# An mLSTM cell feeding a SwiGLU block: TensorE's order written out by hand, and the running maximum fetched by DMA

## The chip, the cores and the metric

The kernel runs on one core of a Trainium2 chip. The metric is the device time in microseconds of one execution. Before the change it was 806.16 us (median of 3 runs, 801.5 to 810.28). The core's engines are TensorE (PE, whose weight loads appear apart as PEld), VectorE (DVE), ScalarE (ACT), GpSimd (POOL) and SyncE (SP), which here issues DMAs.

## The reference

Two blocks follow each other. The first is an mLSTM cell over 4 batches, 8 heads, 768 time steps and a head width of 40, with a running maximum `m` that keeps the exponentials bounded:

```python
for t in range(S):
    m_new = np.maximum(f_gate[:, :, t] + m, i_gate[:, :, t])
    f_stab = np.exp(f_gate[:, :, t] + m - m_new)
    i_stab = np.exp(i_gate[:, :, t] - m_new)
    C = f_stab * C + i_stab * outer(v_t, k_t)
    n = f_stab * n + i_stab * k_t
    y[:, :, t] = sigmoid(o_t) * (C @ q_t) / max(|n . q_t|, 1)
```

The second takes the cell's output as 3072 tokens of width 320 and computes `(silu(x @ w_gate) * (x @ w_val)) @ w_out` with a hidden width of 1536. Everything is float32, except that the three weight matrices arrive as float64.

## The kernel before

**The cell** works in chunks of 128 time steps: 4 batches of 6 chunks, 24 chunks ("units") `u`. Inside a chunk the recurrence becomes matrix products. A chunk passes through `turn` (transposes `tp_kq` of k and q on TensorE; the copy `v_w` of v weighted for the state), `scores` (`sp`, k times q for each head, and a multiplication by the weights `w`), `attend` (`inter`, the state times q; `add`, the chunk's contribution to the state; `intra`, scores times v; their sum `y`), `rows` (the denominator `den`, and `x`, doubled into `xx_sb`) and `seam` (transposes `tp_x` that write x into `xT`). Heads lie in pairs, one in partitions 0 to 63 and one in 64 to 127, so `sp` contracts over 64 rows; it handles the four pairs of one half, and then the four of the other.

**The weights** `w` of a chunk are exp(g - M) under a causal mask, where M is the running maximum found by a scan on VectorE. M must stand in all 128 partitions. `weigh(b)` does that for a whole batch with 48 TensorE products `nm` over 32 rows; VectorE adds g, GpSimd masks, ScalarE takes the exponential.

**The feed-forward** works on half a batch, 384 tokens, at a time. `hidden` computes one of 12 slices of the hidden width: ten products `gv_ps` over 64 rows each, alternately for the gate (partitions 0 to 63) and the value (64 to 127); a sigmoid on ScalarE and two multiplications on VectorE follow. `project` multiplies by `w_out` for 128 tokens: 12 products `o_ps` over 128 rows. A float32 product is two instructions in the trace, a transpose one, so a `hidden` step is 20 rows of `gv_ps` there and a projection 24 of `o_ps`.

**The float64 weights** are converted on the chip in 18 pieces (`weight`), 12 of them for the gate and value and 6 for the output matrix: two raw loads or one, five operations on VectorE, a square on ScalarE, an addition on GpSimd. Three raw buffers turn over.

**Order.** The first batch of the cell is emitted with the conversions between its stages. After that the feed-forward of batch b is emitted with the cell of batch b+1 spread evenly between its steps. A scheduler then places the instructions of every engine, TensorE's too, by its own estimates of when each can run; every engine executes its list in order. SP issues the loads of k, q, v, o and the stores of the result from one in-order list; ScalarE's list issues the raw weight loads.

PSUM is split into four buffers for the cell (`cell`) and four for the feed-forward (`gen`).

Of the kernel before, what the change touches and what calls it, by code (L numbers as in the profile page):

```python
# [9 lines left out]
F32 = mybir.dt.float32  # L10
U32 = mybir.dt.uint32
# [3 lines left out]
PSUM = bass.MemoryType.PSUM  # L15

L = 128
# [4 lines left out]
def kernel(  # L22
# [19 lines left out]

    nc = tc.nc
# [8 lines left out]
    TW = S // 2  # L52
    HP = 64
    NKC = DM // HP
    assert NKC * HP == DM and NB * L == S and NFC * 128 == DF and TW % 128 == 0 and TW <= 512 and D <= DP and BH <= 128

    const = ctx.enter_context(tc.tile_pool(name="const", bufs=1))
    wpool = ctx.enter_context(tc.tile_pool(name="wpool", bufs=1))
    dpool = ctx.enter_context(tc.tile_pool(name="dpool", bufs=NB + 1))
    work = ctx.enter_context(tc.tile_pool(name="work", bufs=2))  # L60
    xtp = ctx.enter_context(tc.tile_pool(name="xtp", bufs=2))
    gsp = ctx.enter_context(tc.tile_pool(name="gsp", bufs=3))
# [10 lines left out]
    NR = 3  # L73
    kq_ring = [const.tile([128, 2, H, DP], F32, name=f"kq{r}") for r in range(NR)]
    v_ring = [const.tile([128, H, D1], F32, name=f"va{r}") for r in range(NR)]
    for r in range(NR):
        nc.vector.memset(kq_ring[r][:, :, :, D:], 0.0)
        nc.gpsimd.memset(v_ring[r][:, :, D:], 1.0)

    units = {}  # L80
    NU = B * NB

    def load(u):
        if u >= NU:
            return
        b, c = divmod(u, NB)
        un = units[u] = {"kq": kq_ring[u % NR], "v": v_ring[u % NR]}
        un["o"] = work.tile([128, H, D], F32, name="o_sb", bufs=NR)

        def src(a):  # L90
            return a[b, :, ts(c, L), :].rearrange("h p d -> p h d")

        nc.sync.dma_start(out=un["kq"][:, 0, :, 0:D], in_=src(k))
        nc.sync.dma_start(out=un["kq"][:, 1, :, 0:D], in_=src(q))
        nc.sync.dma_start(out=un["v"][:, :, 0:D], in_=src(v))
        nc.sync.dma_start(out=un["o"], in_=src(o_gate))

    for u in range(NR - 1):
        load(u)
# [9 lines left out]
    nid = const.tile([BH, BH], F32)  # L109
    nc.vector.tensor_scalar(nid, idb, scalar1=-1.0, scalar2=None, op0=ALU.mult)  # L110
# [8 lines left out]
    own = const.tile([128, 2 * D1], F32)  # L119
    nc.gpsimd.memset(own, 0.0)  # L120
    for two in range(2):
        nc.gpsimd.memset(own[two * DP:(two + 1) * DP, two * D1:(two + 1) * D1], 1.0)
# [3 lines left out]
    step = gates.tile([BH, NB, L], F32)  # L126
    nc.gpsimd.memset(step, 0.0)
# [5 lines left out]
    F_sb = gates.tile([BH, NB, L], F32)  # L133
    nc.vector.tensor_tensor_scan(flat(F_sb), flat(keep), flat(f_sb), 0.0, op0=ALU.mult, op1=ALU.add)
    g_sb = gates.tile([BH, NB, L], F32)
    nc.vector.tensor_sub(g_sb, i_sb, F_sb)
    nc.vector.tensor_copy(step[:, 1:, 0:1], F_sb[:, 0:NB - 1, L - 1:L])
    M_sb = const.tile([BH, NB, L], F32)
    nc.vector.tensor_tensor_scan(flat(M_sb), flat(step), flat(g_sb), NEG, op0=ALU.add, op1=ALU.max)
    m_in = gates.tile([BH, NB - 1, 1], F32)  # L140
# [24 lines left out]
    gates_scope.close()  # L165

# [6 lines left out]
    def weight(dst, src):  # L173
        if src[0][1].dtype == F32:
            for r, s in src:
                nc.scalar.dma_start(out=dst[r], in_=s)
            return
        shape = list(dst.shape)
        n = 1
        for x in shape[1:]:  # L180
            n *= x
        p = shape[0]

        def tmp(name, dt):
            return conv.tile([128, NPW], dt, name=name)[0:p, 0:n]

        raw = conv.tile([128, 2 * NPW], U32, name="raw", bufs=3)[0:p, 0:2 * n]
        for r, s in src:
            nc.scalar.dma_start(out=raw[r].rearrange("p (a d) -> p a d", a=shape[1]), in_=s.bitcast(U32))
        words = raw.rearrange("p (n two) -> p n two", two=2)  # L190
        lo, hi = words[:, :, 0], words[:, :, 1]

        top = tmp("top", U32)
        nc.vector.tensor_scalar(top, hi, scalar1=3, scalar2=0x3FFFFFFF, op0=ALU.logical_shift_left, op1=ALU.bitwise_and)  # L194
        nc.vector.scalar_tensor_tensor(top, in0=hi, scalar=0xC0000000, in1=top, op0=ALU.bitwise_and, op1=ALU.bitwise_or)  # L195
        size = tmp("size", F32)
        nc.scalar.activation(size, hi.bitcast(F32), AF.Square)
        nc.vector.scalar_tensor_tensor(top.bitcast(F32), in0=size, scalar=1.21 * 2.0 ** -30, in1=top.bitcast(F32),  # L198
                                       op0=ALU.is_ge, op1=ALU.mult)

        power = tmp("power", U32)
        nc.vector.tensor_scalar(power, top, scalar1=0xFF800000, scalar2=None, op0=ALU.bitwise_and)
        nc.vector.scalar_tensor_tensor(size, in0=lo, scalar=2.0 ** -52, in1=power.bitcast(F32),  # L203
                                       op0=ALU.mult, op1=ALU.mult)
        sz, tf = (x.rearrange("p (a d) -> p a d", a=shape[1]) for x in (size, top.bitcast(F32)))
        nc.gpsimd.tensor_tensor(dst, tf, sz, op=ALU.add)  # L206

    pieces = []
    for f0 in range(0, DF, PW):
        src = [(slice(i * HP, (i + 1) * HP), w[:, f0:f0 + PW].rearrange("(c p) f -> p c f", p=HP))  # L210
               for i, w in enumerate((moe_w_gate, moe_w_val))]
        pieces.append((wgv_sb[:, :, f0:f0 + PW], src))
    for m in range(0, NFC, 2):
        src = moe_w_out[m * 128:(m + 2) * 128].rearrange("(a p) d -> p a d", p=128)
        pieces.append((wo_sb[:, m:m + 2, :], [(slice(0, 128), src)]))


    w_tiles = {}

# [197 lines left out]
```

## Time and profile before

| what | value |
|---|---|
| profiled execution, its own time | 804.57 us |
| its span, first to last instruction | 802.8 us |
| mean granted TensorE clock | 0.947 |
| PE busy | 750.8 us (94%) |
| DVE busy | 329.1 us (41%) |
| ACT busy | 161.8 us (20%) |
| POOL busy | 132.4 us (16%) |
| HBM read, written | 27.72 MB, 3.93 MB |

Lines such as `L339 PE MATMUL gv_ps<-xT,wgv_sb` name the line of the kernel, the engine, the operation, and output and inputs by the program's names. Busy time counts overlapping instructions once, and the mean duration of one does not. In a list in order of time, the first number is the start in microseconds from the span's beginning and the second the length. In a table of stretches each engine's busy time stands with the number of its instructions, and behind them the granted clock, the DMA engines' busy share and the GB/s.

### The profile page before, as it was taken

How to read it: one execution, taken by the hardware profiler on the slowest of the kernel's cores; microseconds unless marked ns; L12 is line 12 of the kernel's file. 1: busy time of each engine (PE TensorE's matmuls, PEld its weight loads, DVE VectorE, ACT ScalarE, POOL GpSimd, SP SyncE). 2: the span in 40 equal slices, each digit the busy share in tenths (PEclk: the TensorE clock that was granted, in tenths of full speed). 3: DMA queues.
4: the chain of work that ended last, by engine and by line, in shares of the span. 5: the costliest groups of instructions: out<-in, count | busy, mean ns of one | idle time of the engine just before them, and what ended most of it. 6: DMA issues, size and time to landing. Idle time of an engine off the chain costs nothing.

```text
span 802.8 us, 10446 instructions
## 1 busy us (share of the span) xinstructions
PE 750.8 (94%) x4293; PEld 549.6 (68%) x4293; DVE 329.1 (41%) x571; ACT 161.8 (20%) x292; POOL 132.4 (16%) x145
## 2 busy tenths in 40 slices
PE   3956687999999999999999999999999999999998
PEld 2855666697676667976677667966677667556665
DVE  4577799743431442333422442333413441230330
ACT  2322123232202220322201220322201210110110
POOL 1453344431110100210110100310111000000000
PEclk9999997559999999789999999689999999999999
DMA  9266676001120111001110121010110000000000
GB/s 136 58 113 114 115 172 172 18 9 33 26 41 25 34 30 37 17 9 33 33 42 18 33 42 33 9 25 18 33 42 9 1 1 17 9 1 17 9 1 25
DMA packets 113136, 32.34 MB, mean 40 GB/s; under 512 B 100736, under 2 KB 111488, under 8 KB 113088
## 3 DMA queue, kind: packets, MB, share of 16 engines
q1 hardware_dynamic: 103392, 19.87, 14.2%
q10 hardware_dynamic: 9696, 11.80, 6.2%
q8 instruction: 34, 0.56, 0.3%
q14 instruction: 14, 0.11, 0.0%
HBM read 27.72 MB, written 3.93 MB: 39 GB/s over the span
## 4 chain that ended last, share of the span: by engine, by line
PE 91%; DVE 4%; issue 1%; POOL 1%; ACT 0%; ACTq 0%; DVEq 0%; POOLq 0%
PE gv_ps L339 40%; PE o_ps L349 20%; PE nm L228 9%; PE intra L291 6%; PE sp L261 5%; PE tp_kq L250 3%; PE inter L271 3%; PE add L278 3%; PE tp_x L321 2%; DVE top L195 1%; POOL xx_sb L311 1%; DVE top L194 1%; DVE top L198 0%; DVE size L203 0%; POOL wgv_sb L206 0%
## 5 line engine op out<-in xcount | busy, mean ns | idle before, releaser
L339 PE MATMUL gv_ps<-xT,wgv_sb 64*128 64x384 f32 x1920 | 344.4, 497 | 0.0
L339 PEld LDWEIGHTS gv_ps<-xT,wgv_sb 64*128 64x128 f32 x1920 | 191.3, 190 | 117.5 <-issue 12.3
L343 DVE TENSOR_TENSOR sg<-sg,gv_ps 128x384 f32<-128x384 f32 x96 | 53.2, 554 | 286.5 <-ACT sg L342 286.5
L349 PE MATMUL o_ps<-wo_sb,h_sb 128*128 128x320 f32 x576 | 158.7, 435 | 0.0
L349 PEld LDWEIGHTS o_ps<-wo_sb,h_sb 128*128 128x128 f32 x576 | 108.3, 190 | 45.2 <-issue 1.1
L342 ACT ACTIVATE sg<-gv_ps 128x384 f32<-128x384 f32 x96 | 47.0, 489 | 241.6 <-PE gv_ps L339 241.6
L228 PE MATMUL nm<-M_sb,nid 32*128 32x128 f32 x384 | 76.0, 390 | 0.0
L228 PEld LDWEIGHTS nm<-M_sb,nid 32*128 32x128 f32 x384 | 74.9, 301 | 0.7 <-issue 0.3
L245 POOL TENSOR_TENSOR v_w<-va,w_sb 128x328 f32<-128x328 f32 x24 | 18.2, 761 | 244.1 <-PE add L278 206.6
L230 DVE TENSOR_TENSOR w_sb<-nm,g_T 128x512 f32<-128x512 f32 x48 | 33.2, 692 | 61.5 <-PE nm L228 61.5
L344 DVE TENSOR_TENSOR h_sb<-sg,gv_ps 128x384 f32<-128x384 f32 x96 | 53.2, 554 | 11.0 <-PE gv_ps L339 1.2
L291 PE MATMUL intra<-va,s_sb 128*128 128x41 f32 x384 | 52.7, 302 | 0.0
L261 PEld LDWEIGHTS sp<-qT,kT 64*128 64x128 f32 x384 | 44.6, 215 | 11.6 <-ACT qT L252 6.5
L291 PEld LDWEIGHTS intra<-va,s_sb 128*128 128x128 f32 x384 | 51.5, 215 | 1.1 <-DVE top L198 1.1
L261 PE MATMUL sp<-qT,kT 64*128 64x128 f32 x384 | 46.0, 309 | 4.3 <-ACT qT L252 4.3
L321 PE MATMUL tp_x<-ident,xx_sb 128*128 128x128 f32 x120 | 21.4, 318 | 30.5 <-POOL xx_sb L311 30.5
L308 POOL TENSOR_TENSOR x_sb<-o_sb,y_sb 128x320 f32<-128x320 f32 x24 | 22.6, 941 | 155.4 <-DVE y_sb L294 151.1
L321 PEld LDWEIGHTS tp_x<-ident,xx_sb 128*128 128x128 f32 x120 | 15.6, 160 | 41.1 <-POOL xx_sb L311 33.3
L232 POOL TENSOR_SCALAR_AFFINE_SELECT w_sb<-w_sb 128x1024 f32<-128x1024 f32 x24 | 27.6, 1152 | 80.1 <-DVE w_sb L230 80.1
L352 ACT COPY z_sb<-o_ps 128x320 f32<-128x320 f32 x24 | 10.2, 426 | 137.2 <-PE o_ps L349 137.2
L234 ACT ACTIVATE w_sb<-w_sb 128x1024 f32<-128x1024 f32 x24 | 25.4, 1057 | 54.7 <-POOL w_sb L232 54.7
L301 ACT ACTIVATE o_sb<-o_sb 128x320 f32<-128x320 f32 x24 | 11.2, 468 | 114.0 <-DMA o_sb<-in_o_gate_dram 114.0
(67 smaller groups left out, 495.6 us busy)
## 6 DMA issues: line engine op xcount, KB each, us to landing
kq<-in_k_dram SPq DMA_DIRECT2D x24, 160.0 KB, 3.0
kq<-in_q_dram SPq DMA_DIRECT2D x24, 160.0 KB, 3.1
va<-in_v_dram SPq DMA_DIRECT2D x24, 160.0 KB, 2.6
o_sb<-in_o_gate_dram SPq DMA_DIRECT2D x24, 160.0 KB, 2.5
raw<-in_moe_w_gate_dram ACTq DMA_DIRECT2D x12, 320.0 KB, 5.0
raw<-in_moe_w_val_dram ACTq DMA_DIRECT2D x12, 320.0 KB, 4.5
raw<-in_moe_w_out_dram ACTq DMA_DIRECT2D x6, 640.0 KB, 5.3
out_dram<-z_sb SPq DMA_DIRECT2D x24, 160.0 KB, 1.8
```

The source lines that it names most:

```text
L228: nc.tensor.matmul(nm[:, j, :], lhsT=nid[:, row:row + 1].to_broadcast([BH, 128]), rhs=M_sb[:, c, :], start=True, stop=True)
L230: nc.vector.tensor_tensor(w[:, two], nm, g2[:, two].unsqueeze(2).to_broadcast([128, PR, L]), op=ALU.add)
L232: nc.gpsimd.affine_select(wf, wf, compare_op=ALU.is_ge, fill=NEG, base=0, pattern=[[0, H], [1, L]], channel_multiplier=-1)
L234: nc.scalar.activation(wf, wf, AF.Exp)
L261: nc.tensor.matmul(sp[:, j, :], lhsT=un["kT"][r, j, :], rhs=un["qT"][r, j, :], start=True, stop=True)
L291: nc.tensor.matmul(intra[:, h, :], lhsT=un["s"][:, h % 2, h // 2, :], rhs=un["v"][:, h, :], start=True, stop=True)
L321: nc.tensor.transpose(tp[:, kc - k0, :], units[u]["x"][:, kc, :, :].rearrange("p a d -> p (a d)"), ident)
L339: nc.tensor.matmul(ps[i], lhsT=wgv_sb[r, kc, ts(m, 128)], rhs=xts[b][r, kc, ts(n, TW)], start=(kc == 0), stop=(kc == NKC - 1))
L342: nc.scalar.activation(sg, ps[0], AF.Sigmoid)
L343: nc.vector.tensor_tensor(sg, sg, ps[0], op=ALU.mult)
L344: nc.vector.tensor_tensor(hs[b, n][:, m, :], sg, ps[1], op=ALU.mult)
L349: nc.tensor.matmul(p, lhsT=hs[b, n][:, m, ts(i, 128)], rhs=wo_sb[:, m, :], start=(m == 0), stop=(m == NFC - 1))
```

## The change

The program is reorganized around groups of three chunks, 384 tokens, the size of one feed-forward pass; there are eight groups.

- **TensorE's order is written down.** The scheduler still places the other engines, but TensorE executes in the order of emission. For each group `g`: the 12 hidden steps of `g`, with the scores of the three chunks of group `g+1` after steps 1, 4 and 7; then the projections of `g` in nine parts of four products each, with `attend` and `seam` of group `g+1` and the transposes (`turn`) of group `g+2` between the parts.
- **The maximum goes by DMA.** M is written to DRAM once, and each chunk loads it back into all partitions (512 KB per chunk); VectorE forms g - M in SBUF. The `nm` products and the batch-wide `weigh` are gone; `weigh` now works chunk by chunk, two groups ahead.
- **Scores alternate halves**: head pair 0 of one half, pair 0 of the other, pair 1 of the one, and so on, into two PSUM buffers.
- **The multiplication by the weights** goes in place into `w`. The state is kept in two buffers whose foreign blocks stay zero, so that it is formed by two additions on half the partitions each rather than by a multiplication with a mask and an addition. `rows` is part of `attend`.
- **The conversions** write into the weight tiles directly, use two raw buffers instead of three, load through SP instead of ScalarE, and are spread as six pieces before the first hidden step, nine during group 0's hidden phase and three at its end.
- k and q lie in separate rings of six and four buffers, v in six; the hidden results are single slices in 13 buffers.

```diff
+    tc_order = ctx.enter_context(tc.manual_schedule(engines={PE}))
...
+    M_dram = tc.dram_tile([BH, S], F32, name="M_dram")
+    nc.sync.dma_start(out=M_dram, in_=flat(M_sb))
...
-            nc.scalar.dma_start(out=raw[r].rearrange("p (a d) -> p a d", a=shape[1]), in_=s.bitcast(U32))
+            nc.sync.dma_start(out=raw[r].rearrange("p (a d) -> p a d", a=shape[1]), in_=s.bitcast(U32))
...
-                for j in range(PR):
-                    row = b * H + 2 * j + two
-                    nc.tensor.matmul(nm[:, j, :], lhsT=nid[:, row:row + 1].to_broadcast([BH, 128]), rhs=M_sb[:, c, :],
-                                     start=True, stop=True)
-                nc.vector.tensor_tensor(w[:, two], nm, g2[:, two].unsqueeze(2).to_broadcast([128, PR, L]), op=ALU.add)
...
+        w = un["w"] = work.tile([128, H, L], F32, name="w_sb", bufs=2 * GC - 1)
+        src = M_dram[b * H:(b + 1) * H, ts(c, L)].unsqueeze(0).to_broadcast([128, H, L])
+        nc.sync.dma_start(out=w, in_=src)
+        gb = g_T[:, c, b * H:(b + 1) * H].unsqueeze(2).to_broadcast([128, H, L])
+        nc.vector.tensor_tensor(w, gb, w, op=ALU.subtract)
...
+        for j in range(PR):
+            for two in range(2):
+                r = slice(two * DP, two * DP + DP)
+                nc.tensor.matmul(sps[two][:, j, :], lhsT=un["kT"][r, j, :], rhs=un["qT"][r, j, :], start=True, stop=True)
...
+    for g in range(NG):
+        nxt, after = list(group(g + 1)), list(group(g + 2))
...
+        for m in range(NFC):
+            if g == 0 and m + 3 < NFC:
+                convert(1)
+            hidden(g, m)
+            if nxt and m % 3 == 1 and m // 3 < GC:
+                scores(nxt[m // 3])
+        if g == 0:
+            convert(len(pieces))
...
+        for u in after:
+            weigh(u)
...
+            follow = {-1: [(attend, nxt[0])], 1: [(attend, nxt[1])], 3: [(attend, nxt[2])],
+                      4: [(seam, nxt[0])], 5: [(seam, nxt[1])], 7: [(seam, nxt[2])]}
+        for n, u in zip((4, 5, 6), after):
+            follow.setdefault(n, []).append((turn, u))
+        for n in range(-1, 3 * GC):
+            if n >= 0:
+                project(g, *divmod(n, 3))
+            for f, u in follow.get(n, ()):
+                f(u)
```

In TensorE's list before, a hidden phase of a later batch reads as follows; counts are products, and numbers behind k, v and kq are buffers.

```order
L228 MATMUL nm<-M_sb,nid 128x128 x48
L339 MATMUL gv_ps<-xT,wgv_sb 128x384 x10
L250 MATMUL tp_kq<-ident,kq_83 128x128 x8
L339 MATMUL gv_ps<-xT,wgv_sb 128x384 x10
L261 MATMUL sp<-qT,kT 128x128 x8
L339 MATMUL gv_ps<-xT,wgv_sb 128x384 x10
L278 MATMUL add<-v_w,kq_83 128x82 x4
L291 MATMUL intra<-va_86,s_sb 128x41 x8
L339 MATMUL gv_ps<-xT,wgv_sb 128x384 x20
L321 MATMUL tp_x<-ident,xx_sb 128x128 x5
```

In TensorE's list now, the same place, from the start of a group's hidden phase into its projections:

```order
L327 MATMUL gv_ps<-xT,wgv_sb 128x384 x20
L252 MATMUL sp<-qT,kT 128x128 x8
L327 MATMUL gv_ps<-xT,wgv_sb 128x384 x30
L252 MATMUL sp<-qT,kT 128x128 x8
L327 MATMUL gv_ps<-xT,wgv_sb 128x384 x30
L252 MATMUL sp<-qT,kT 128x128 x8
L327 MATMUL gv_ps<-xT,wgv_sb 128x384 x40
L272 MATMUL add<-v_w,k_82 128x82 x4
L290 MATMUL intra<-v_92,w_sb 128x41 x8
L342 MATMUL o_ps<-wo_sb,h_sb 128x320 x8
L265 MATMUL inter<-C_136,qT 128x82 x4
```

The `nm` block is gone, only scores stand between the `gv_ps`, and the cell's 128-row products have moved in between the projections.

On VectorE, near the end of the conversions in the startup, the list before alternates conversion steps (`top`, `power`, `size`) with the last chunks of the first batch:

```order
L198 SCALAR_TENSOR_TENSOR top<-size,top 128x640
L343 TENSOR_TENSOR sg<-sg,gv_ps 128x384
L202 TENSOR_SCALAR power<-top 128x640
L194 TENSOR_SCALAR top<-raw 128x640
L203 SCALAR_TENSOR_TENSOR size<-raw,power 128x640
L262 TENSOR_TENSOR s_sb<-sp,w_sb 128x512 x2
```

On VectorE now, the end of the conversions (`wo_sb` is the output matrix, `raw` and `size` are scratch):

```order
L331 TENSOR_TENSOR sg<-sg,gv_ps 128x384
L205 SCALAR_TENSOR_TENSOR size<-raw 128x640
L333 TENSOR_TENSOR h_sb<-sg,gv_ps 128x384
L198 TENSOR_SCALAR wo_sb<-raw 128x640
L199 SCALAR_TENSOR_TENSOR wo_sb<-raw,wo_sb 128x640
L202 SCALAR_TENSOR_TENSOR wo_sb<-size,wo_sb 128x640
L204 TENSOR_SCALAR raw<-wo_sb 128x640
L205 SCALAR_TENSOR_TENSOR size<-raw 128x640
L331 TENSOR_TENSOR sg<-sg,gv_ps 128x384
L333 TENSOR_TENSOR h_sb<-sg,gv_ps 128x384
```

The chunks of the cell have left this place; hidden steps of group 0 stand between the conversions, and the last conversion stands ahead of the last two of them.

298 lines of the change are left out of this document (143 added, 155 removed).

## The prediction

> **What bounds the kernel now.** I read the page first (busy shares, then the chain of waits), then the chain in order of time, then two stretches by engine, then TensorE's instructions in order.
>
> ```profile
> PE 750.8 (94%) x4293; PEld 549.6 (68%) x4293; DVE 329.1 (41%) x571; ACT 161.8 (20%) x292; POOL 132.4 (16%) x145
> PE 91%; DVE 4%; issue 1%; POOL 1%; ACT 0%; ACTq 0%; DVEq 0%; POOLq 0%
> 18.00:38.00 20.00, 20.00 (x95) 19.78 (x95) 10.70 (x17) 5.95 (x6) 8.15 (x8) 1.00 0.35 81
> 38.00:158.00 120.00, 85.20 (x418) 72.77 (x416) 99.65 (x146) 31.40 (x54) 49.99 (x39) 0.87 0.58 118
> 328.00:505.00 177.00, 177.00 (x1068) 127.07 (x1066) 62.07 (x116) 35.95 (x68) 23.32 (x28) 0.95 0.15 29
> ```
>
> The last three rows are stretches of the span: length, then busy time of PE, PEld, DVE, ACT, POOL, then granted clock, DMA share and GB/s. There are two regimes. From 38 to 158 us VectorE is busy 99.65 of 120 us: it converts the weights, and PE waits. From then on PE is busy 177.00 of 177 us, and only TensorE's own time counts. The longest pieces of the chain, start and length first:
>
> ```profile
> 16.09 20.57 PE nm L228 x96
> 153.21 20.78 PE nm L228 x96
> 327.41 17.05 PE nm L228 x96
> 344.46 5.46 PE gv_ps L339 x20
> 350.94 3.43 PE gv_ps L339 x20
> 505.05 17.18 PE nm L228 x96
> 682.69 38.90 PE gv_ps L339 x240
> 721.59 19.58 PE o_ps L349 x72
> 780.07 19.59 PE o_ps L349 x72
> ```
>
> A group of 384 tokens costs 38.90 us of `gv_ps` and 19.58 us of `o_ps` when nothing stands between. Four batches pay about 17 to 21 us each for `nm`, the broadcast of the maximum. The prices of the other products come from the starts of successive rows of PE (start, length, instruction):
>
> ```profile
> 215.05 3.50 PE L339 MATMUL gv_ps<-xT,wgv_sb 64*128 64x384 f32 x20
> 218.48 1.09 PE L250 MATMUL tp_kq<-ident,kq 128*128 128x128 f32 x8
> 219.50 3.50 PE L339 MATMUL gv_ps<-xT,wgv_sb 64*128 64x384 f32 x20
> 222.83 1.60 PE L261 MATMUL sp<-qT,kT 64*128 64x128 f32 x16
> 224.37 6.73 PE L349 MATMUL o_ps<-wo_sb,h_sb 128*128 128x320 f32 x24
> 230.93 1.02 PE L271 MATMUL inter<-C_sb,qT 128*128 128x82 f32 x8
> 231.78 1.06 PE L278 MATMUL add<-v_w,kq 128*128 128x82 f32 x8
> 232.68 1.92 PE L291 MATMUL intra<-va,s_sb 128*128 128x41 f32 x16
> 234.42 13.17 PE L349 MATMUL o_ps<-wo_sb,h_sb 128*128 128x320 f32 x48
> 247.42 0.71 PE L321 MATMUL tp_x<-ident,xx_sb 128*128 128x128 f32 x5
> 248.06 3.50 PE L339 MATMUL gv_ps<-xT,wgv_sb 64*128 64x384 f32 x20
> ```
>
> Per chunk of 128 tokens: tp_kq 1.02, sp 1.54, inter 0.85, add 0.90, intra 1.74, tp_x 0.64 us.
>
> **The change, part by part.** *The maximum by DMA.* The 384 `nm` instructions go. On the saturated path that is 20.78 + 17.05 + 17.18 = 55.0 us; the first 20.57 us lie in the startup, below. What follows an `nm` block is slow too (5.46 us for 20 `gv_ps` at 344.46, 3.43 six us later: 2.0 us). In their place come 24 DMAs of 512 KB and, on VectorE, a subtraction of 128x1024 in SBUF. After saturation both lie beside PE.
>
> *Scores in alternating halves.* `o_ps` takes 19.58/72 = 0.272 us for 320 columns, so 384 columns would take 0.326; a `gv_ps`, half the rows, takes 38.90/240 = 0.162, just half. So two 64-row products in different halves run side by side at full rate. Scores of before run one half after the other: 16 in 1.54 us. Alternating, 8 steps of 128 columns at 0.272/320 us a column are 0.87 us; I take 0.9. The bounds are 0.77 (half of 1.54) and 1.54 (no gain). 21 chunks on the saturated path x 0.64 = 13 us.
>
> *Phases.* A `gv_ps` block of 20 between other work takes 3.43 us start to start, a twelfth of the long run 38.90/12 = 3.24: about 0.2 us for each break. Before has some five breaks a group, after has one, with the scores (64 rows as well) as three interruptions of 0.09 us (3.33 - 3.24, the row at 219.50). About 5 us in all.
>
> *A steady group now:* 38.90 + 19.58 + 3 x (1.02 + 1.74 + 0.64) + 2.5 x (0.85 + 0.90) for inter and add, which the first and last chunk of a batch lack, + 3 x 0.9 + 0.44 for breaks = 76.2 us. Groups 1 to 5 are such: 381.0. Group 6 has no transposes for a group after next: 73.1. Group 7 is bare: 58.5. Group 0 from the end of its hidden phase: 34.3. Together 546.9.
>
> *The startup* ends when VectorE has converted all 18 weight pieces: in the new order every conversion stands ahead of the last two hidden steps. Its work:
>
> ```profile
> L195 DVE SCALAR_TENSOR_TENSOR top<-raw,top x18: 805/818/2085, 27.1 to 152.8; 128x640 uint32<-128x640 uint32 x18
> 59.08 1.76 POOL L206 TENSOR_TENSOR wgv_sb<-top,size 128x640 f32<-128x640 f32 x1 [3.08 <-DVE size L203]
> 59.44 2.08 DVE L195 SCALAR_TENSOR_TENSOR top<-raw,top 128x640 uint32<-128x640 uint32 x1
> L230 DVE TENSOR_TENSOR w_sb<-nm,g_T 128x512 f32<-128x512 f32 x48 | 33.2, 692 | 61.5 <-PE nm L228 61.5
> L309 DVE TENSOR_TENSOR x_sb<-x_sb,den 128x320 f32<-128x320 f32 x24 | 11.8, 490 | 1.9
> L343 DVE TENSOR_TENSOR sg<-sg,gv_ps 128x384 f32<-128x384 f32 x96 | 53.2, 554 | 286.5 <-ACT sg L342 286.5
> raw<-in_moe_w_gate_dram ACTq DMA_DIRECT2D x12, 320.0 KB, 5.0
> kq<-in_k_dram SPq DMA_DIRECT2D x24, 160.0 KB, 3.0
> ```
>
> From 18 to 158 us VectorE worked 10.70 + 99.65 = 110.4 us. After has nearly the same sum. The same 18 conversions. Twelve score multiplies either way. The weighing of eight chunks: two `nm` additions of 0.69 each become one subtraction; from 0.490 for 320 and 0.692 for 512 columns, an estimate of 1.23 us for 1024. Three chunks fewer through the cell, eight operations near 0.49 us each: -11.8. Ten hidden steps more of 2 x 0.554: +11.1. So 110 us again, from 18 us on: the first maximum has to go to DRAM and come back, which no row shows; nearest rows 3.0 and 5.0 us to land, and the scan ends early enough for 18.
>
> What changes is the idle time. Before, VectorE idled 9.3 us of 18 to 38 behind `nm`; that goes. From 38 to 158 it idled 17%, behind three more chunks than there are now, but now there are two raw buffers instead of three, and a load takes 5.0 us after its buffer is freed. I keep 17%: 110.4/0.83 = 133, so PE leaves the hidden phase of group 0 at about 151 us. Bounds: no idle, 128 (I hold 136 for the lowest that a real order reaches), and 167 with a quarter idle.
>
> **The sum.** 151 + 546.9 + the end after the last matmul (802.8 - 799.7 = 3.1) = 701; 4 us for short waits in a written order: 705 us of span. The profiled execution took 804.57 for a span of 802.8, so 707; it lay 0.2% under the median 806.16, which I leave.
>
> **What speaks against it.** That 2.08 us beside POOL's 1.76, for an operation whose middle value is 0.818, is a wait for POOL, up to 2.08 - 0.82 = 1.3 us. The subtraction reads SBUF twice, where the addition of before read PSUM; if each of the eight in the startup met such a wait, 10 us would be added, and the sum were 717. I leave it out of the middle, since POOL is busy 49.99 of 120 us, and count it with the longer startup below. The Trainium skill, "SBUF — State Buffer", section "SBUF: two separate sides", says that a VectorE operation with two SBUF inputs and a GpSimd operation that reads SBUF shut each other out for a whole instruction; by that rule, the trace agrees, and the subtraction newly falls under it.
>
> PE's clock matters in the startup too: it was granted 0.87 from 38 to 158 us, where PE waits. Of VectorE's 155 instructions in the new startup 55 stand ahead of the third chunk's last one, so the hidden steps start near 18 + 133 x 55/155 = 65 us. At half clock all through, twelve would take 12 x 2 x 3.24 = 78 us, to 143: covered by VectorE's 151, and the bound if they start 8 us later.
>
> **The rivals.**
> - *Scores don't pair* (the change doesn't do what it says): 21 x 0.64 = 13 more, 720. For: each product loads its weights first. Against: `gv_ps` does pair.
> - *The maximum lands late.* SP's queue is in order; the load for the third chunk of a group stands behind stores and loads that wait for the projection phase. Subtraction, select and exponential follow, and on ScalarE the copies of `kT` and `xT` stand behind that exponential, so hidden step 0 waits. I count some 5 us of slack, if a load lands in 4. At the rate of 160 KB in 3.0 us, 512 KB take 9.8, so 5 us a group for six groups: 735.
> - *Startup longer*: waits for POOL, two buffers and half a clock, 167: 723. *Shorter*: 136: 692.
> - *Slower than before.* PE's order is fixed, so a product that waits holds everything behind it. The place is `tp_x` behind `o_ps`: it needs the chain from `intra` over y, x and `xx_sb`.
>
> ```profile
> 56.06 1.33 PE L321 MATMUL tp_x<-ident,xx_sb 128*128 128x128 f32 x5 [6.87 <-POOL xx_sb L311]
> ```
>
> With nothing to cover it, that chain stops PE for 6.87 us. Three chunks in six groups, uncovered, are 124 us: 831. It decides once a group waits over (806 - 707)/6 = 16.5 us. Against it: the order puts 20 products of `o_ps`, 40 x 0.272 = 10.9 us, and two more chunks between the first chunk's `intra` and its `tp_x`.
>
> **How the numbers follow.** Chances: the forecast 0.55; scores unpaired 0.10; late maximum 0.13; longer startup 0.12, shorter 0.06; slower 0.04, of which 0.01 ends within 1%. The time is the likeliest, 707. The range runs from 686 (shorter startup, scores at 0.77) to 738 (the late maximum, or longer startup and unpaired scores together); it leaves out the slow case and parts of the late maximum. One per cent, 8 us, is about what a measurement tells from no change. Faster 0.95, same 0.02, slower 0.03.
>
> **What would show it.** `gv_ps` of all groups after the first in 38.9 us plus three breaks; 16 `sp` in about 0.9 us; no `nm` and a granted clock of 1.00 from 160 us on; PE's first `o_ps` near 151 us, with VectorE over 80% busy before it; each steady group near 76 us. Wrong, if PE shows waits of several us ahead of `gv_ps` after a projection phase (late maximum) or ahead of `tp_x`, or if the first `o_ps` comes after 170 us.

## The result, and the profile after

| | median | lowest to highest |
|---|---|---|
| before, measured beside it | 808.22 us | 801.5 to 811.01 |
| the changed kernel | 701.83 us | 701.29 to 702.75 |

The ratio is 0.8695 (95% interval 0.8637 to 0.8754): 13% faster. Predicted were 707 us, with 686 to 738 as the range. The profiled execution took 701.29 us for a span of 699.5. One execution, of the experiment with the later subtraction, lay in a slower state and is left out there.

From the page of the changed kernel, the busy shares of the engines, and the shares of the chain of waits:

```profile
PE 644.2 (92%) x3909; PEld 457.6 (65%) x3909; DVE 324.7 (46%) x557; ACT 190.8 (27%) x317; POOL 130.9 (19%) x143
PE 81%; DVE 10%; issue 4%; ACT 2%; POOL 2%; DMA 2%; SPq 0%; DVEq 0%; POOLq 0%; ACTq 0%
```

The span fell by 802.8 - 699.5 = 103.3 us. PE's busy time fell by 750.8 - 644.2 = 106.6 us; its idle time went from 52.0 to 55.3 us. In the chain DVE has 10% where it had 4%: more of the startup is put down to VectorE. So the gain is work taken out of TensorE's list, and on balance no waiting went. Which work, the groups of TensorE's instructions show, first of before and then of the changed kernel (after the bar: busy us, mean ns; then idle time before them).

```profile
L339 PE MATMUL gv_ps<-xT,wgv_sb 64*128 64x384 f32 x1920 | 344.4, 497 | 0.0
L349 PE MATMUL o_ps<-wo_sb,h_sb 128*128 128x320 f32 x576 | 158.7, 435 | 0.0
L228 PE MATMUL nm<-M_sb,nid 32*128 32x128 f32 x384 | 76.0, 390 | 0.0
L261 PE MATMUL sp<-qT,kT 64*128 64x128 f32 x384 | 46.0, 309 | 4.3 <-ACT qT L252 4.3
```

```profile
L327 PE MATMUL gv_ps<-xT,wgv_sb 64*128 64x384 f32 x1920 | 334.9, 497 | 26.7 <-DVE sg L331 23.3 <-DVE h_sb L333 3.3
L342 PE MATMUL o_ps<-wo_sb,h_sb 128*128 128x320 f32 x576 | 165.0, 436 | 0.0
L252 PE MATMUL sp<-qT,kT 64*128 64x128 f32 x384 | 29.6, 292 | 6.0 <-DVE w_sb L255 6.0
```

The 76.0 us of `nm` are most of it. The scores `sp` lost 16.4 and the hidden products `gv_ps` 9.5 us; the projections `o_ps`, now cut into nine parts, gained 6.3.

The changed kernel by stretches, with PE, PEld, DVE, ACT and POOL, then clock, DMA share and GB/s:

```profile
18.00:38.00 20.00, 10.42 (x67) 9.02 (x65) 14.86 (x19) 7.83 (x10) 7.43 (x7) 0.70 0.89 171
38.00:98.00 60.00, 46.29 (x247) 40.68 (x248) 43.02 (x65) 20.64 (x32) 26.31 (x22) 0.67 1.00 164
98.00:158.00 60.00, 42.23 (x182) 22.91 (x181) 55.71 (x73) 14.72 (x22) 22.47 (x15) 0.83 0.40 105
158.00:300.00 142.00, 142.00 (x917) 100.71 (x918) 58.59 (x108) 45.08 (x74) 23.03 (x28) 1.00 0.27 58
```

The two regimes are still there. From 18 to 158 us VectorE works 14.86 + 43.02 + 55.71 = 113.6 of 140 us and PE waits; from 158 us on PE is busy without a gap, at clock 1.00 (the same holds from 300 to 690 us). TensorE's list, from the end of the startup and through a steady group (start, length, instruction):

```profile
151.74 3.49 PE L327 MATMUL gv_ps<-xT,wgv_sb 64*128 64x384 f32 x18 [0.23 <-DVE h_sb L333]
155.16 1.12 PE L265 MATMUL inter<-C,qT 128*128 128x82 f32 x8
...
158.75 4.55 PE L342 MATMUL o_ps<-wo_sb,h_sb 128*128 128x320 f32 x16
...
188.83 6.72 PE L327 MATMUL gv_ps<-xT,wgv_sb 64*128 64x384 f32 x40
...
205.95 1.06 PE L252 MATMUL sp<-qT,kT 64*128 64x128 f32 x16
206.84 9.84 PE L327 MATMUL gv_ps<-xT,wgv_sb 64*128 64x384 f32 x60
...
230.41 1.12 PE L272 MATMUL add<-v_w,k 128*128 128x82 f32 x8
```

PE leaves group 0's hidden phase at 155.16 us. The next group begins at 188.83; in the chain of waits the starts of later groups lie 75.25 us apart (188.90, 264.15 and so on to 565.16). Sixteen `sp` take 205.95 to 206.84, 0.89 us, and a hidden phase 230.41 - 188.83 = 41.58 us, which is 38.90 + 3 x 0.89 with nothing left for breaks.

### The profile page after: what moved, and what is told of

Read it like the earlier page. It is cut to its first block, busy times and chain, and to the rows that moved or that the text cites. A ratio compares the mean times of both kernels' runs of the same rounds, so it can differ in the third digit from the quotient of the medians.

```text
span 699.5 us, 9732 instructions
## 1 busy us (share of the span) xinstructions
PE 644.2 (92%) x3909; PEld 457.6 (65%) x3909; DVE 324.7 (46%) x557; ACT 190.8 (27%) x317; POOL 130.9 (19%) x143
## 4 chain that ended last, share of the span: by engine, by line
PE 81%; DVE 10%; issue 4%; ACT 2%; POOL 2%; DMA 2%; SPq 0%; DVEq 0%; POOLq 0%; ACTq 0%
PE gv_ps L327 40%; PE o_ps L342 22%; PE intra L290 6%; PE add L272 3%; PE inter L265 3%; PE sp L252 2%; PE tp_kq L242 2%; PE tp_x L315 2%; DVE wgv_sb L199 1%; DVE size L205 1%; DMA raw<-in_moe_w_val_dram 1%; DVE raw L204 1%; POOL w_sb L230 1%; DVE wo_sb L199 1%; DVE wgv_sb L198 1%
## 5 line engine op out<-in xcount | busy, mean ns | idle before, releaser
L290 PE MATMUL intra<-v,w_sb 128*128 128x41 f32 x384 | 50.9, 297 | 1.2 <-issue 1.2
L290 PEld LDWEIGHTS intra<-v,w_sb 128*128 128x128 f32 x384 | 49.8, 210 | 1.4 <-issue 1.4
L235 POOL TENSOR_TENSOR v_w<-v,w_sb 128x328 f32<-128x328 f32 x20 | 16.0, 802 | 159.5 <-ACT sg L330 148.8
L280 POOL TENSOR_TENSOR kept<-C,dec 128x328 f32<-128x328 f32 x16 | 13.5, 845 | 166.2 <-DVE C L284 164.8
L229 DVE TENSOR_TENSOR w_sb<-g_T,w_sb 128x1024 f32<-128x1024 f32 x24 | 32.0, 1340 | 25.8 <-DMA w_sb<-M_dram 25.8
L252 PEld LDWEIGHTS sp<-qT,kT 64*128 64x128 f32 x384 | 28.6, 205 | 12.0 <-DVE w_sb L255 6.6
L252 PE MATMUL sp<-qT,kT 64*128 64x128 f32 x384 | 29.6, 292 | 6.0 <-DVE w_sb L255 6.0
L255 DVE TENSOR_TENSOR w_sb<-sp,w_sb 128x512 f32<-128x512 f32 x48 | 31.2, 682 | 0.6 <-POOL v_w L235 0.6
L206 POOL TENSOR_TENSOR wgv_sb<-wgv_sb,size 128x640 f32<-128x640 f32 x12 | 20.9, 1739 | 45.1 <-DVE size L205 43.9
L316 ACT COPY xT<-tp_x 128x512 f32<-128x512 f32 (+1 forms) x48 | 18.2, 432 | 35.9 <-PE tp_x L315 35.9
L265 PEld LDWEIGHTS inter<-C,qT 128*128 128x128 f32 x160 | 22.2, 205 | 7.0 <-DVE C L284 2.6
```

The costliest lines, as they stand in the source:

```text
L229: nc.vector.tensor_tensor(w, gb, w, op=ALU.subtract)
L252: nc.tensor.matmul(sps[two][:, j, :], lhsT=un["kT"][r, j, :], rhs=un["qT"][r, j, :], start=True, stop=True)
L255: nc.vector.tensor_tensor(w2[:, two], sps[two], w2[:, two], op=ALU.mult)
L265: nc.tensor.matmul(inter[:, 2 * j:2 * j + 2, :].rearrange("p h d -> p (h d)"), lhsT=un["qT"][:, j, :], rhs=old[:, j].rearrange("p a d -> p ...
L290: nc.tensor.matmul(intra[:, h, :], lhsT=un["w"][:, h, :], rhs=un["v"][:, h, :], start=True, stop=True)
```

## Experiments

The theory on trial: after the startup only the sum of TensorE's own instructions counts, and the maximum, the pairing of the scores and the fewer breaks each took their price out of it; before that, VectorE's conversions set the end. The rivals: the parts are worth something else than priced, or it is the written order itself that gains.

### Scores by halves again

```diff
-        for j in range(PR):
-            for two in range(2):
+        for two in range(2):
+            for j in range(PR):
```

> The changed kernel, with the scores back in the old order: the four pairs of one half, then the four of the other. Theory (two 64-row products in different halves run side by side): 16 rows of sp take 1.54 us again where they now take 0.9, so a steady group goes from 75.25 to 77.2 us, and 21 chunks on the saturated path cost 13 us: about 715 us against 702. Rival (products this short are bound by their weight loads, and the 0.9 us come from their place between gv_ps): no change, 702.

Measured: 708.83 us (708.24 to 709.45), 7.0 over the changed kernel, half of the price; the rival, no change, is out. The starts of steady groups lie 76.24 us apart, 0.33 us a chunk more and not 0.64. On 18 chunks that is 5.9 us; the other part lies in the startup, where the first `o_ps` comes at 160.28 us instead of 158.75. TensorE's list of this kernel, around a chunk's scores:

```profile
273.14 1.27 PE L252 MATMUL sp<-qT,kT 64*128 64x128 f32 x13
274.14 0.59 PE L327 MATMUL gv_ps<-xT,wgv_sb 64*128 64x384 f32 x1
274.25 0.49 PE L252 MATMUL sp<-qT,kT 64*128 64x128 f32 x3
274.57 9.53 PE L327 MATMUL gv_ps<-xT,wgv_sb 64*128 64x384 f32 x58
```

The last scores of one half run side by side with the first `gv_ps` of the other: by 274.57 us two `gv_ps` are already through. So a block of one half loses less than its length when a product of the other half stands next. The 1.54 us that I had read in before stood ahead of `o_ps`, a product over all 128 rows, and there none overlapped. Of the 18 chunks that before has behind its second `nm` block, 6 stand ahead of `o_ps`. The other 12 stand ahead of `gv_ps` and overlap it as here. In before, for one, thirteen `sp` begin at 199.25 us, and this row stands between them and the last three:

```profile
200.25 0.59 PE L339 MATMUL gv_ps<-xT,wgv_sb 64*128 64x384 f32 x1
```

### Four more breaks in each hidden phase

The transposes of two chunks of the group after next move from between the projections into the hidden phase, one block of four each behind hidden steps 2, 3, 5 and 6:

```diff
...
             hidden(g, m)
...
+            if len(after) and m in (2, 3, 5, 6):
+                turn_half(after[0 if m < 4 else 1], 0 if m in (2, 5) else 1)
...
-        for n, u in zip((4, 5, 6), after):
+        for n, u in zip((6,), after[2:]):
```

> The changed kernel, with the transposes of two of the three chunks of the group after next taken out of the projection phase and put, k and q apart, between hidden steps: four more breaks of the 64-row run in each of the groups 0 to 5, the same products. Theory (a break costs 0.2 us): a steady group goes from 75.25 to 76.0 us, the whole by 4 us to 706. Rival (a change between 64 and 128 rows drains the engine and costs 1 us or more, and the phases are what the change gained by): 4 us or more a group, 725 or above.

Measured: 709.66 us (708.55 to 710.52). The starts of steady groups lie 76.66 us apart, 1.41 more for four breaks: 0.35 us each, where I had taken 0.2. That is far from the rival's 4 us a group. The startup ends later too (first `o_ps` at 162.25 us instead of 158.75), so the total doesn't price the breaks, the distance of groups does.

### The maximum by TensorE again, in the new order

```diff
-        src = M_dram[b * H:(b + 1) * H, ts(c, L)].unsqueeze(0).to_broadcast([128, H, L])
-        nc.sync.dma_start(out=w, in_=src)
         gb = g_T[:, c, b * H:(b + 1) * H].unsqueeze(2).to_broadcast([128, H, L])
-        nc.vector.tensor_tensor(w, gb, w, op=ALU.subtract)
+        for a in range(2):
+            nm = psum.tile([128, PR, L], F32, name="nm", tag="cell")
+            for j in range(PR):
+                row = b * H + 4 * a + j
+                nc.tensor.matmul(nm[:, j, :], lhsT=nid[:, row:row + 1].to_broadcast([BH, 128]), rhs=M_sb[:, c, :],
+                                 start=True, stop=True)
+            nc.vector.tensor_tensor(w[:, 4 * a:4 * a + 4], nm, gb[:, 4 * a:4 * a + 4], op=ALU.add)
```

> The changed kernel, with the maximum broadcast by TensorE again: 8 nm products for each chunk, in blocks of three chunks between the hidden phase and the projections, added from PSUM by VectorE; no M in DRAM. Theory (the products cost what they stream, 16 rows of 0.109 us, 1.74 us a chunk, and 18 chunks lie on the saturated path): 31 us more, 733, and a granted clock near 1.00 still, as a block of 5.2 us is short. Rival (32-row products bring the clock down to half as in the kernel before): 2.8 us a chunk and slow products behind each block, 60 us more, 762. The startup may shorten by some us, as no chunk waits for its DMA.

Measured: 760.54 us (756.77 to 762.86), 58.7 over the changed kernel. A steady group takes 86.05 us on the mean of five, 10.8 more, though a group's 48 `nm` instructions take 6 us. TensorE's list and then the granted clock (the column behind the count) from the block on:

```profile
232.00 6.01 PE L231 MATMUL nm<-M_sb,nid 32*128 32x128 f32 x48
237.94 2.00 PE L276 MATMUL add<-v_w,k 128*128 128x82 f32 x8
239.73 3.55 PE L294 MATMUL intra<-v,w_sb 128*128 128x41 f32 x16
```

```profile
234.00:236.00 2.00, 2.00 (x20) 1.00 0.00 0
236.00:238.00 2.00, 2.00 (x16) 0.77 0.00 0
238.00:240.00 2.00, 2.00 (x11) 0.50 0.00 0
...
248.00:250.00 2.00, 2.00 (x12) 1.00 0.37 67
```

The clock falls to half between 4 and 6 us into the block, while PE is busy the whole time, and comes back some 10 us later, 9 us after the block's end. What stands there pays for it: `add` takes 2.00 us instead of 1.06, `intra` 3.55 instead of 1.92.

### The same in short bursts

From the third group on, a chunk's 16 `nm` instructions go between two parts of the projection, rather than three chunks on end:

```diff
-        for u in after:
-            weigh(u)
...
+        for n, u in zip((0, 2, 6), after):
+            follow.setdefault(n, []).append((weigh, u))
```

> As e3_max_by_tensor, where TensorE makes the maximum's row again, but from the third group on its 32-row products stand in bursts of one chunk (16 instructions, about 1.74 us) between parts of the projection, not in blocks of three chunks (5.9 us); nothing is left out. Theory that the clock falls only after some 4 us of 32-row products on end: the granted clock stays at 1.00 in the steady groups, a group costs 5.2 us of products and some 1 to 2 us of breaks over 75.25, and the time is 735 to 742. Rival, that any 32-row products lower the clock: the clock falls again and the time is about 760.

Measured: 732.68 us (732.48 to 734.34), as the theory has it: 27.9 us less than with blocks. A steady group takes 81.72 us, 6.47 over the changed kernel. A burst begins at 244.45 us, and the clock doesn't move, then or later:

```profile
244.00:246.00 2.00, 2.00 (x16) 1.00 0.71 130
246.00:248.00 2.00, 2.00 (x11) 1.00 0.20 69
...
250.00:300.00 50.00, 50.00 (x337) 1.00 0.16 31
```

So of the 58.7 us that the maximum by TensorE costs in the new order, about 28 come from issuing it in blocks. The other 31 are not the whole price of the products with their breaks. Six groups at 6.47 us are 38.8, and the startup gives 7.5 of them back: the hidden phase of group 0 ends at 147.64 us here and at 155.16 in the changed kernel (with blocks at 146.30). There the maximum first goes to DRAM and back, for which VectorE waits 8.02 us, until 19.35 us, and the subtractions read SBUF beside GpSimd; how much of the 7.5 us each of the two costs, no run separates.

### The scheduler's order in place of the written one

```diff
-    tc_order = ctx.enter_context(tc.manual_schedule(engines={PE}))
```

> The changed kernel without its written order for TensorE: the scheduler places TensorE too, from the same sequence of emission. Theory (the phases come from the sequence in which the steps are emitted, and the fixed order by itself is worth nothing): 702 within 4 us. Rival (the fixed order is what keeps the phases together): 5 breaks a group return and 702 grows by 6 us or more.

Measured: 697.22 us (696.47 to 697.5), 4.6 us less than with the written order, a little more than the theory allowed. Steady groups are 75.25 us apart as before; the first `o_ps` comes at 154.61 us instead of 158.75. Writing the order down gains nothing: the phases come from the sequence in which the program emits its work, and the scheduler keeps them. What it places better in the startup, no run takes apart.

### The maximum by DMA alone, in the kernel before

```diff
+    M_dram = tc.dram_tile([BH, S], F32, name="M_dram")
+    nc.sync.dma_start(out=M_dram, in_=flat(M_sb))
...
             for two in range(2):
-                nm = psum.tile([128, PR, L], F32, name="nm", tag="cell")
...
+                nc.sync.dma_start(out=w[:, two], in_=src[two].unsqueeze(0).to_broadcast([128, PR, L]))
...
+            nc.vector.tensor_tensor(w, gb, w, op=ALU.subtract)
```

> The kernel before with one part of the change alone: the maximum goes to DRAM and comes back by DMA, and VectorE subtracts in SBUF; no nm products, everything else as before. Theory (the three later nm blocks lie on the saturated path, 55.0 us, what follows them is slowed by 2 us or more each, and the startup loses VectorE's 9 us of waiting): 808 falls by about 70 us to 738. Rival (the gain turns into waits for the DMAs, eight products of time for 512 KB each, since the batch's six chunks are all weighed at its start): above 760.

Measured: 791.02 us (787.55 to 795.4), ratio 0.983 (0.976 to 0.9901). PE's busy time fell from 750.8 to 684.5 us, but the span by 17 only. Rows of its list of waits (us in total, times, longest):

```profile
DVE w_sb L230 <- DMA w_sb<-M_dram: 65.0, 19, 6.1
PE tp_x L321 <- POOL xx_sb L311: 47.0, 7, 12.6
PE gv_ps L339 <- DVE sg L343: 17.9, 9, 2.5
```

PE in two stretches, of before and then of this kernel:

```profile
0.00:200.00 200.00, 151.18 (x765) 0.87 0.50 94
```

```profile
0.00:200.00 200.00, 117.23 (x632) 0.86 0.69 134
200.00:780.00 580.00, 564.75 (x3271) 0.99 0.14 31
```

In the first 200 us before had two `nm` blocks, 20.57 + 20.78 = 41.4 us; without them PE idles 82.8 us instead of 48.8, so 34 of the 41 came back as waiting. After 200 us it now waits 15.3 us, where before had no gap. Together 49.3 us of new waits, which is what is missing: 66.3 - 49.3 = 17.0. VectorE stands 65.0 us behind loads of the maximum. After 200 us PE stands behind VectorE's `sg`, for 15.0 of the 15.3 us. In the first 200 us other waits grew: `tp_x` behind `xx_sb` to 47.0 us in all from 30.5 in before, and `add` behind `v_w` (7.0) and `intra` behind `s_sb` (5.5) are new. That these too come from the loads, the rows don't show.

### The subtraction moved behind its load, in the kernel before

The kernel of the last experiment, with VectorE's subtraction, the mask and the exponential of a chunk emitted one chunk ahead of its use:

```diff
+    def prep(u):
...
+            nc.vector.tensor_tensor(w, gb, w, op=ALU.subtract)
...
-        return [(f, u) for u in us for f in (turn, scores, attend, rows, seam)]
+        stages = [(prep, us[0])]
+        for u in us:
+            stages += [(turn, u), (scores, u)]
+            if u + 1 in us:
+                stages += [(prep, u + 1)]
+            stages += [(attend, u), (rows, u), (seam, u)]
+        return stages
```

> The kernel before with the maximum taken through the DMA, as in e8_before_max_by_dma, and VectorE's subtraction, the mask and the exponentials of a chunk moved one chunk ahead of their use, while the DMA is still issued at the batch's start; nothing is left out. Theory that e8's gain went into VectorE standing behind freshly issued DMAs (65 us there): the waits on w_sb<-M_dram fall below 10 us and the time comes to about 740. Rival, that the rest of the order before eats the gain whatever the maximum does: the DMA waits go but others take their place, and the time stays near 785.

Measured: 791.05 us (784.4 to 795.13). The time is the rival's, but the experiment doesn't decide, because the wait that it was to remove is still there. From its list in order of time:

```profile
315.82 1.29 DVE L268 TENSOR_TENSOR s_sb<-sp,w_sb 128x512 f32<-128x512 f32 x2 [6.84 <-PE sp L267]
317.14 0.92 SPq L228 DMA_DIRECT2D w_sb<-M_dram  x2
321.69 1.23 DVE L236 TENSOR_TENSOR w_sb<-g_T,w_sb 128x1024 f32<-128x1024 f32 x1 [4.58 <-DMA w_sb<-M_dram]
```

The load goes out when the scores' multiplication has freed its buffer, at 317.11 us, and the subtraction of the same chunk stands next in VectorE's list: VectorE's order is the scheduler's, and it pulled the subtraction forward again, seven chunks ahead of its use. These waits add up to 59.3 us, against 65.0. Whether the order before would keep the gain with a later subtraction stays open.

### The startup: the second load group later

In group 0, the output gates of group 1 and the k, q and v of group 2 are loaded ahead of hidden steps 6 and 9 (counted from 0) rather than ahead of step 0:

```diff
-        for u in nxt:
-            load_o(u)
-        for u in after:
-            load(u)
+        if g > 0:
+            for u in nxt:
+                load_o(u)
+            for u in after:
+                load(u)
         for m in range(NFC):
+            if g == 0 and m == 6:
+                for u in nxt:
+                    load_o(u)
+            if g == 0 and m == 9:
+                for u in after:
+                    load(u)
```

> The changed kernel, with two loads of group 0's hidden phase moved: the o gates of group 1 and their sigmoid from ahead of the first hidden step to ahead of the seventh, and k, q, v of group 2 to ahead of the tenth. Theory (VectorE's pause from 72 to 81 us is ScalarE's: its first hidden sigmoid stands behind three exponentials and three sigmoids of o with four table loads between them, and DMAs are saturated at that time): the first sigmoid comes some 6 us earlier, the first o_ps near 151 us instead of 158.7, 695 us in all. Rival (the startup is bound by VectorE's work alone): 702.

Measured: 695.84 us (695.43 to 695.91), as expected; first `o_ps` at 153.35 us, where 151 was expected. The wait that it mends stands at the start of the changed kernel's first hidden phase. These rows show ScalarE there, and the last row VectorE, which waits for it:

```profile
76.35 1.28 ACT L232 ACT_TABLE_LOAD   x1
...
78.72 1.28 ACT L109 ACT_TABLE_LOAD   x1
80.01 0.83 ACT L109 ACTIVATE o_sb<-o_sb 128x320 f32<-128x320 f32 x2
80.75 0.85 ACT L330 ACTIVATE sg<-gv_ps 128x384 f32<-128x384 f32 x2
81.25 1.02 DVE L331 TENSOR_TENSOR sg<-sg,gv_ps 128x384 f32<-128x384 f32 x2 [8.74 <-ACT sg L330]
```

Output gates that are needed only in the projections stand ahead of the first hidden sigmoid, with table loads of 1.28 us between them and the exponentials. VectorE, which has 113.6 us to do, stands for 8.74 us. With the gates loaded later, its first `sg` begins at 76.13 us. The loads of k, q and v were moved in the same run; what each of the two moves is worth alone, it doesn't show.

### The startup: conversions on contiguous rows

Each piece of `wgv_sb` lies in five runs of 128. VectorE's one-input steps take 0.81 us on it and 0.49 on the contiguous `wo_sb`. A first try wrote the intermediate steps into a contiguous scratch tile, alone and together with the later loads:

```diff
...
-        top = dst.bitcast(U32)
+        tt = conv.tile([128, NPW], U32, name="top", bufs=1)[0:p, 0:n].rearrange("p (a d) -> p a d", a=shape[1])
+        top = tt
...
```

> The changed kernel, with the conversion's intermediate words in a contiguous scratch tile again and not in five runs of 128 in the weight tile (12 instead of 13 buffers for the hidden results make room). Theory (VectorE bounds the startup, and its two one-input operations take 0.81 us on the five runs and 0.48 on contiguous words): 12 pieces x 0.66 = 8 us of VectorE go, the first o_ps comes 5 to 8 us earlier, 695 us. Rival (waits, not work, bound the startup): 702.

> Both edits, the late loads and the contiguous scratch. If both theories hold and the gains add: 688 us, the first o_ps near 144 us. If one bound hides behind the other: 695.

Measured: 704.14 us (703.71 to 704.61) and 702.32 us (700.72 to 702.79), no gain over 701.83 and a loss over 695.84. There was room for one scratch buffer, and VectorE waited for GpSimd's addition to leave it, as the list of waits of the first of the two shows for 18 to 160 us:

```profile
DVE top L198 <- POOL wgv_sb L207: 11.1, 8, 2.1
```

So these two say nothing on what contiguous rows are worth.

A second try changed the layout of the weights themselves, and needs no scratch (`PW0` is 128):

```diff
-    wgv_sb = wpool.tile([128, NKC, DF], F32)
+    wgv_sb = wpool.tile([128, NFC, NKC, PW0], F32)
...
-                nc.tensor.matmul(ps[i], lhsT=wgv_sb[r, kc, ts(m, 128)], rhs=xts[g][r, kc, :],
+                nc.tensor.matmul(ps[i], lhsT=wgv_sb[r, m, kc, :], rhs=xts[g][r, kc, :],
```

> The changed kernel with the group projection's weights laid out so that each converted piece is one contiguous run per partition; nothing is left out. Theory that VectorE's work bounds the startup: 12 + 12 conversions at 0.48 instead of 0.81 us take about 8 us off VectorE, the first o_ps comes 5 to 8 us earlier than 158.75, and the time is about 695. Rival, that arrival of the weights or ScalarE bounds it: first o_ps within 2 us of 158.75 and 702.

Measured: 698.06 us (696.89 to 698.76), 3.8 us less; first `o_ps` at 155.48 us. That is between the two expectations, and the reason is in the durations. The same step, in the changed kernel and then here (least, median, most ns):

```profile
L198 DVE TENSOR_SCALAR wgv_sb<-raw x12: 762/812/820, 23.6 to 120.0; 128x640 uint32<-128x640 uint32 x12
```

```profile
L199 DVE TENSOR_SCALAR wgv_sb<-raw x12: 429/484/1826, 23.2 to 116.8; 128x640 uint32<-128x640 uint32 x12
```

```profile
97.19 2.45 POOL L207 TENSOR_TENSOR wgv_sb<-wgv_sb,size 128x640 f32<-128x640 f32 x1 [1.63 <-DVE size L206]
98.16 1.83 DVE L199 TENSOR_SCALAR wgv_sb<-raw 128x640 uint32<-128x640 uint32 x1
```

The median fell as priced, but in its slower form the step was never held, and in the faster one it can be: at 98.16 us it lies beside GpSimd's addition and takes 1.83 us, ending 0.35 us behind it. VectorE's busy time from 18 us on is the same in both, 113.6 us to 158 and 114.1 us to 155. By groups of instructions, the one-input steps on `wgv_sb` fell from 19.5 to 14.6 us, and the two-input steps of the conversions rose from 52.9 to 57.5, so what the layout saved was lost again beside them. The 3.3 us by which the first `o_ps` comes earlier are idle time of VectorE. The Trainium skill, "SBUF — State Buffer", section "SBUF: two separate sides", says that VectorE in a mode that uses both ports and GpSimd exclude each other for whole instructions; by that, the trace agrees, if the faster form is such a mode.

### What beats both

The later loads, the contiguous layout and the scheduler's order together:

> The changed kernel with the loads of the second group's maximum issued later (as in e4_late_loads), the contiguous weight layout (as in e10_contiguous_layout) and the scheduler's order in place of the written one (as in e7_scheduler_order); nothing is left out. If the three gains are separate (6.0, 5 to 8 and 4.6 us) the time is 684 to 688; if they remove the same wait of VectorE and ScalarE in the startup, it is 692 to 696. The steady group stays at 75.25 us in both.

Measured: 693.7 us (693.0 to 694.52), ratio to before 0.8591 (0.8546 to 0.8636); first `o_ps` at 151.98 us. Apart, the three gained 6.0, 3.8 and 4.6 us; together 8.1. They are largely remedies for the same idle time of VectorE in the startup. This is the fastest of the kernels here, 1.2% under the changed one.

### The maximum, in either organization

| | maximum by TensorE | maximum by DMA | difference |
|---|---|---|---|
| order before | 804.52 | 791.02 | 13.5 (ratio 0.983, interval 0.976 to 0.9901) |
| new organization, products in blocks | 760.54 | 701.83 | 58.7 |
| new organization, products in bursts | 732.68 | 701.83 | 30.9 |

Against products in blocks, as the order before has them, the maximum by DMA is worth some four times as much in the new organization; against products in bursts, some twice as much. Down the first column, the rest of the change is worth some 44 us with the products in blocks. In the new organization too VectorE waits behind loads just issued, as this row of the changed kernel's VectorE shows:

```profile
254.89 1.23 DVE L229 TENSOR_TENSOR w_sb<-g_T,w_sb 128x1024 f32<-128x1024 f32 x1 [2.07 <-DMA w_sb<-M_dram]
```

But this is the projection phase (230.41 to 264 us), for which the hidden steps are all done, and PE stays busy. In the order before, the weighing falls among hidden steps, whose PSUM buffers come free only through VectorE. That this makes the difference is argued, not shown.

## Why the prediction was right, and where not

The sum was 151 for the startup, 546.9 for the groups, 3.1 for the end and 4 for short waits: 705 us of span. Measured: 155.2, then 699.5 - 155.2 = 544.3 for the groups and the end together, no short waits: 699.5. The errors are +4, -6 and -4 us, so part of the closeness is that they cancel. Three numbers beside the sum are off, without effect: a quarter idle would end the startup at 18 + 110.4/0.75 = 165 us and not 167, the shorter startup with scores at 0.77 gives 692 - 2.7 = 689, not the 686 of the range, and 512 KB at 160 KB in 3.0 us are 9.6 us, not 9.8.

- **The steady group** was right: 75.25 us against 76.2. Group 0's projections took 188.83 - 155.16 = 33.7 us (34.3 predicted), and from 565.16 us to the end it was 134.3 (73.1 + 58.5 + 3.1 = 134.7). The regime was named rightly: in the changed kernel and in the experiments on its startup alone (later loads, both conversions, the scheduler's order, the best kernel), the time from the first `o_ps` to the end is 540.7 or 540.8 us.
- **The parts against the whole.** The sum is built from the stages of the new order, so the prices of what was taken out (55, 13 and 5 us) are not terms of it, and their errors did not show in the time. What they should have been, one batch shows: in before it took 505.05 - 327.41 = 177.6 us, two steady groups take 150.5 now, 27.1 less. Of these `nm` is 17.1, what follows it about 2.0, the scores about 2.6 (4 chunks at 0.33, 2 at 0.65); the other 5 or so are the fewer breaks and whatever else the order changed, which no run takes apart.
- **The maximum.** Its price of 55 us on the saturated path and 2 us for each slow follower fits in the new organization (58.7), but part of this agreement is chance. Of the block at 153 us, 20.78 of the 55, and the one before it, 34 of 41 us came back as waiting when they were taken out alone; and about 28 of the 58.7 are what blocks cost over bursts, which I had not priced beyond the followers. That the gain needs the rest of the change, the prediction didn't say: the expectation made of its prices for the maximum alone was 738 us, and measured were 791.
- **Scores.** The pairing was right, 0.89 us against 0.9. The worth was mis-sized: undoing it cost 7.0 us, 5.9 of them after the startup, and not 13. The 1.54 us came from a block ahead of `o_ps`, and ahead of `gv_ps` the blocks of before overlapped; and 18 chunks lie on the saturated path, not 21, since those of groups 0 and 1 are scored in the startup. Against before that makes an estimate of 12 x 0.33 + 6 x 0.65 = 8 us.
- **Phases.** The term of 0.2 us a break was mis-sized: 0.35. Where only scores stand between `gv_ps`, the break that I had added (0.44 a group) costs nothing.
- **The startup** came 4 us late. VectorE's idle share of 17% was nearly right (19% from 18 to 158 us), its work 3 us more. The first maximum came back for 19.35 us, not 18. One term was missing, ScalarE's queue: I had weighed POOL and the raw buffers as what could hold VectorE, and the longest wait after the first maximum was 8.74 us behind ScalarE. The later loads took 5.4 us off the first `o_ps`.
- **What spoke against it** was there, small: at 66.79 us three subtractions took 5.72 us, not 3 x 1.23, beside GpSimd's work:

```profile
66.79 5.72 DVE L229 TENSOR_TENSOR w_sb<-g_T,w_sb 128x1024 f32<-128x1024 f32 x3
69.36 4.10 POOL L230 TENSOR_SCALAR_AFFINE_SELECT w_sb<-w_sb 128x1024 f32<-128x1024 f32 x2
```

  Over all 24 the mean is 1.34 us, where I had estimated 1.23.
- **The rivals.** The late maximum didn't come in the steady groups, where PE waits for nothing; 512 KB landed in 5.2 us in the median, where the rival had taken 9.8. The slower case didn't either: no `tp_x` behind `o_ps` waits. The scores paired. Of the waits that I had named, only those of the startup came.

## What to carry over

Price a removed instruction by the stage it stands in: the same 384 products were worth 13.5 us in one organization, where waits took most of their place, and 58.7 or 30.9 in the other, as they stood in blocks or in bursts. A block between two kinds of work is not priced by its length alone; what stands behind it can overlap it, or pay for it in clock. And look at the stage that is not the target: the last 8 us here were in the startup, in part behind an engine that the forecast had not weighed.

## What the runs showed of the hardware

- The clock fell to half while PE was busy all the time, 4 to 6 us into a run of `nm`, products over 32 rows. It came back 9 us after a block of 48 instructions (the changed kernel with the products put back) and 4 us after a block of 96. Before shows the latter, a block from 327.41 to 344.39 us:

```profile
328.00:330.00 2.00, 2.00 (x20) 1.00 0.23 82
...
332.00:334.00 2.00, 2.00 (x11) 0.50 0.00 0
...
348.00:350.00 2.00, 2.00 (x11) 0.87 0.00 0
```

  Bursts of 2 us with 128-row products between them left it at 1.00. The Trainium skill, "TensorE: Matmul & The Clock Gate", "Part 1: The HAM clock gate", ties the half clock to windows of about 3.4 us in which PE was idle. Here PE was busy throughout, so the measurement differs, unless such products count as little activity; whether it is the 32 rows, no run here separates. The column is not to be trusted at the very start: in before the first block takes 20.57 us at a clock given as 1.00 and the second 20.78 us at 0.50, so both ran at half pace.
- A 64-row product runs beside one of the other half even where they belong to different steps: a `gv_ps` began among the last `sp` at 274.14 us, and the overlap left 0.33 of the 0.65 us that a chunk's unpaired scores cost. A change from 64-row to 128-row work and back cost about 0.35 us (76.66 against 75.25 us for four).
- A VectorE step that becomes faster by its layout can become one that GpSimd holds up: 0.81 us and never over 0.82 with five runs of 128, against a median of 0.48 and up to 1.83 us contiguous.
